# Output projection: a fifth pair of tiles in place of tiles 8 and 9, single steps for the down weights, four buffers for their sums

## The chip, the core and the metric

The kernel runs on one core of one Trainium2 chip. The metric is device time in microseconds (us), as the median of several runs. Engines are named as in the profile: PE (TensorE, matmul), PEld (its weight load), DVE (VectorE), ACT (ScalarE), POOL (GpSimd), SP (SyncE, which here only issues DMAs; SPq is its queue).

## What is computed

The input is one sequence of S = 2048 rows of D = 640. A layer norm feeds two branches whose product is added to the input.

```python
x = A_x
xn = _layernorm(x, axis=-1)
s = _A_ref(xn, A_wqkv, A_wo)
g = _silu(_B_ref(xn, B_w_gate, B_w_up, B_w_down))
return x + s * g
```

Branch A is an attention with 32 heads of 20 columns over 8 positions (every second row back), followed by the output projection `o @ wo` with a 640 x 640 matrix. Branch B is a gated bilinear layer, `((xn @ w_gate) * (xn @ w_up)) @ w_down`, with F = 1536.

```python
attn = _softmax(logits, axis=-1)
o = jnp.einsum("bhsw,bhswd->bhsd", attn, vg)
return (lambda x, *d: x.transpose(*d))(o, 0, 2, 1, 3).reshape(B, S, D) @ wo
```

## The kernel before

**Stages.** The 2048 rows are 16 tiles of 128. First come the norm, the products for q, k, v, the attention on DVE, and the gate and up products (to about 557 us of the span). Then comes the output projection of all 16 tiles (to about 626 us), which is the stage that the change touches. Last come the products with `w_down`, in seven half products for each pair of tiles, with the gate and the output.

**Precision.** A matrix is split in a high part (a copy in the matmul's format, by ACT) and a low part (the matrix less the high part, by DVE or POOL; `split`, L84). A product is then three: high by high, high by low, low by high. The low part of the data comes last, so `mm3` (L91) needs it only for the last third of its matmuls.

**Two forms of the output projection.** Tiles 0 to 7 run as four pairs (`pair_product`, L771). A pair is a 2 x 2 block product done in seven products (numbered 0 to 6, "product (p, j)" for pair p) in place of eight, over 4 of the 5 row blocks of `wo`; the fifth block is added to four of them. A product is 6 matmuls of 320 columns, or 9 with the fifth block. The products accumulate in three PSUM banks, "ACACABA"; the first three are copied to `o` by ACT in between, and a product that adds to the same bank comes behind that copy. Tiles 8 to 15 run singly (`out_proj`, L513): two halves of 15 matmuls of 320 columns each, each evicted by ACT.

**What has to be ready.** For a pair: `load_pair` (four DMAs on SP's queue), `turn_pair` on DVE (two transposes and four sums of 256 columns, L738 to L741), and three high parts (`hi_pair`, ACT) and low parts (`lo_pair`, DVE): part 0 of the first tile, part 2 of the sums S1, S2, S4, part 1 of the second tile. For a single tile: a load (`load_o`), one transpose (`turn_o`, L485), and a high and a low part (`split_o`, L500).

**The down weights beside it.** In the same stage `w_down` is prepared for the last one: 6 blocks k, each in two steps (k, 0) and (k, 1). A step has two sums on DVE (`sum_wd`: L561 and L562, or L566 and L567) and then three or four splits (`split_wd`), high on ACT and low on POOL, 42 in all. The sums T1, T2 stand in tiles of the tag `lg` (two buffers), T4 in `e` (one), so a sum waits until POOL has read what stood there. The attention's logits and two kept products of the last stage use the tag `lg` too.

**Order.** Every engine works its instructions in the order in which the program writes them; nothing is reordered. In pairs 0 to 3 there were 1, 1, 1 and 2 steps of the down weights, and one with each single tile 8 to 14. The tile names that stand in the rows below: `o`, `gs`, `hs` hold outputs on their way to memory, `ot` transposed data, `t` loaded data, `wf` high and low parts, `xc` and `kv` large areas that the down weights and the parts of the pairs share.

Of the kernel before, what the change touches and what calls it, by code (L numbers as in the profile page):

```python
# [37 lines left out]
SCALE = DH ** -0.5  # L38
MASKED = -1e9 / SCALE
EPS = 1e-5  # L40
SP = NT // 2
PAIRS = range(0, W, 2)
PACE = 1.0

# [7 lines left out]
def kernel(  # L52
# [23 lines left out]
    def st(shape, tag, bufs, dt=F32):  # L76
        cnt[0] += 1
        return sb.tile(shape, dt, tag=tag, bufs=bufs, name=f"{tag}_{cnt[0]}")
# [243 lines left out]
    def attention(u):  # L322
        g, r = UN[u]
        nh = GROUPS[g]
        c = nh * DH
        q, kv = q_t[u], kv_t[u]
        pair, one, small = [(n + 155) / 950 for n in (2 * NE * c, NE * c, NE * nh * W)]
        lg = st([P, NE * nh, W], "lg", 2)
        e = st([P, NE * nh, W], "e", 1)
        yield 1.0  # L330

        def places(a, j):

            y = kv[:, a, j:j + NE, :].rearrange("p i c -> p (i c)")
            return bass.AP(y.tensor, y.offset, [y.ap[0], [c, 2], y.ap[1]])

        def pair_tile():
            return st([P, 2, NE * c], "t", 2)

        def heads(y):  # L340
            return y.rearrange("p a (n d) -> p a n d", d=DH)

        for j in PAIRS:
            t = pair_tile()
            nc.vector.tensor_mul(t, q.rearrange("p i c -> p (i c)").unsqueeze(1).to_broadcast([P, 2, NE * c]),  # L345
                                 places(0, j))
            yield pair
            nc.vector.tensor_reduce(out=lg[:, :, j:j + 2].rearrange("p n a -> p a n"), in_=heads(t),  # L348
                                    op=ALU.add, axis=AX.X)
            yield pair  # L350
        m0 = lg[0:1].rearrange("p (i h) w -> p i h w", h=nh)
        nc.vector.tensor_add(m0, m0, mask.unsqueeze(2).to_broadcast([1, NE, nh, W]))
        sm = st([P, 2, NE * nh], "sm", 2)
        nc.vector.tensor_reduce(out=sm[:, 0, :], in_=lg, op=ALU.max, axis=AX.X)
        nc.vector.tensor_sub(lg, lg, sm[:, 0, :].unsqueeze(2).to_broadcast([P, NE * nh, W]))
        yield 3 * small
        nc.scalar.activation(e, lg, AF.Exp, scale=SCALE)
        yield small
        nc.vector.tensor_reduce(out=sm[:, 0, :], in_=e, op=ALU.add, axis=AX.X)
        nc.vector.reciprocal(sm[:, 1, :], sm[:, 0, :])  # L360
        nc.vector.tensor_mul(e, e, sm[:, 1, :].unsqueeze(2).to_broadcast([P, NE * nh, W]))
        yield 3 * small

        def weighted(j, t):
            pw = e[:, :, j:j + 2].rearrange("p n a -> p a n").unsqueeze(3).to_broadcast([P, 2, NE * nh, DH])
            nc.vector.tensor_mul(heads(t), pw, heads(places(1, j)))  # L366

        acc, t = pair_tile(), pair_tile()
        weighted(PAIRS[0], acc)
        yield pair  # L370
        for j in PAIRS[1:]:
            weighted(j, t)
            yield pair
            nc.vector.tensor_add(acc, acc, t)  # L374
            yield pair
        o = st([P, NE, c], "o", 1)
        nc.vector.tensor_add(o.rearrange("p i c -> p (i c)"), acc[:, 0, :], acc[:, 1, :])
        yield one
        for b in range(NQ):
            c0, c1 = max(GOFF[g], b * QC), min(GOFF[g] + c, (b + 1) * QC)  # L380
            if c0 < c1:
                nc.sync.dma_start(o_scr[r, b, :, :, c0 - b * QC:c1 - b * QC].rearrange("s p c -> p s c"),
                                  o[:, :, c0 - GOFF[g]:c1 - GOFF[g]])
# [116 lines left out]
    def split_o(s, y):  # L500
        if s == NT - 2:
            oT[s] = st([P, KD, P], "hs", 2, F32R), st([P, KD, P], "hs", 2, F32R)
        else:
            if s == SP:
                z = blocks(wd_kv["B22"], 4, 2, KD)
            else:
                z = st([P, 2, KD, P], *(("wf", 4) if s < NT - 2 else ("t", 2)), F32R)
            oT[s] = z[:, 0], z[:, 1]
        split(nc.vector, y, *oT[s])
# [46 lines left out]
    def sum_wd(k, part):  # L556
        r = wd_raw[k]
        if part == 0:
            v = wd_v[k] = {"B11": r[:, 0, 0], "B21": r[:, 1, 0], "B22": r[:, 1, 1]}
            v["T1"], v["T2"] = st([P, HALF], "lg", 2), st([P, HALF], "lg", 2)  # L560
            nc.vector.tensor_sub(v["T1"], r[:, 0, 1], r[:, 0, 0])  # L561
            nc.vector.tensor_sub(v["T2"], r[:, 1, 1], v["T1"])  # L562
        else:
            v = wd_v[k]
            v["T4"], v["T3"] = st([P, HALF], "e", 1), r[:, 0, 1]
            nc.vector.tensor_sub(v["T3"], r[:, 1, 1], r[:, 0, 1])  # L566
            nc.vector.tensor_sub(v["T4"], r[:, 1, 0], v["T2"])  # L567
# [89 lines left out]
    def gather(m):  # L657

        n, j = divmod(m, 7)
        a, b = 2 * n, 2 * n + 1  # L660
        p = bank["ACACABA"[j]]
        if j == 0:
            keep("M1", p, "lg", 2)
        elif j == 1:
            keep("M5", p, "lg", 2)
        elif j == 2:
            keep("U2", p, "e", 1)
        elif j == 3:
            g_t[a] = st([P, D], "q", 2)
            nc.vector.tensor_add(g_t[a][:, HALF:], kept["U2"], p)  # L670
            return lambda: silu(a, 1)
        elif j == 4:
            g_t[b] = st([P, D], "q", 2)
            nc.vector.tensor_add(g_t[b][:, HALF:], kept["M5"], p)
            return lambda: silu(b, 1)
        elif j == 5:
            nc.vector.tensor_add(g_t[a][:, :HALF], kept["M1"], p)
            return lambda: silu(a, 0)
        else:
            return lambda: silu(b, 0, p)  # L680
        return lambda: None
# [61 lines left out]
    def hi_pair(p, part):  # L743

        if part == 2:
            if p % 2:
                z = [st([P, 2, KD, P], "wf", 4, F32R).rearrange("p a k c -> p (a k) c")[:, :3 * KS] for _ in range(2)]
            else:
                z = blocks(wd_kv["T4"], 2, 2, 3 * KS) if p else blocks(wd_big[0], 1, 2, 3 * KS)
                z = [z[:, 0], z[:, 1]]  # L750
            raw = pair_raw[p]
        else:
            y, r = (wd_big[3], 3) if p % 2 else (wd_kv["B22"], 2) if p else (wd_kv["T4"], 1)
            z = blocks(y, r, 2, 2 * KD)
            z = [z[:, i, part * KD:(part + 1) * KD] for i in range(2)]
            raw = pair_y[p][:, part]
        pair_z[p, part] = z, raw
        nc.scalar.activation(z[0], raw, AF.Copy)
# [219 lines left out]
    pair_k.append(st([P, 3, HALF], "o", 1))  # L978
    wd_steps = [(k, part) for k in range(KH) for part in range(2)]

    def wd_sums(n):
        for k, part in wd_steps[:n]:
            sum_wd(k, part)

    def wd_splits(n):
        for k, part in wd_steps[:n]:
            split_wd(k, part)
            if part and k + 2 < KH:
                load_wd(k + 2)
        del wd_steps[:n]  # L990

    pair_product(0, 0)
    for p in range(SP // 2):
        more = p + 1 < SP // 2
        n = (1, 1, 1, 2)[p]
        if not more:
            y8 = turn_o(SP)
        wd_sums(n)
        pair_product(p, 1)
        if more:  # L1000
            hi_pair(p + 1, 0)
            lo_pair(p + 1, 0)
        else:
            split_o(SP, y8)
        pair_product(p, 2)
        if more:
            hi_pair(p + 1, 2)
        pair_product(p, 3)
        if more:
            lo_pair(p + 1, 2)  # L1010
            hi_pair(p + 1, 1)
        pair_product(p, 4)
        wd_splits(n)
        if more:
            lo_pair(p + 1, 1)
        pair_product(p, 5)
        if p == 0:
            load_pair(3)
        elif p == 1:
            load_o(SP, 3, st([P, 3, D], "t", 2))  # L1020
            turn_pair(3)
        elif p == 2:
            load_o(SP + 3, 3, st([P, 3, D], "t", 2))
        if more:
            pair_product(p + 1, 0)
        else:
            out_proj(SP, 0)
        pair_product(p, 6)
    n_prod = 7 * NT // 2
    for s in range(SP, NT):  # L1030
        if s + 1 < NT:
            trans_o(s + 1)
        if s == SP + 2:
            load_o(SP + 6, 2, st([P, 2, D], "t", 2))
        wd_sums(1)
        if s > SP:
            out_proj(s, 0)
        out_proj(s, 1)
        wd_splits(1)
        if s == 12:  # L1040
            load_h(0, ("A11", "A21", "A12"))
        elif s == 13:
            load_h(0, ("A22",))
        if s == 14:
            hi_h(0)
            lo_h(0)
# [76 lines left out]
```

## Time and profile before

| what | value |
|---|---|
| median of 3 runs | 779.98 us (779.87 to 781.29) |
| profiled execution | 779.86 us |
| its span | 778.0 us, granted TensorE clock 0.999 |
| output projection, first to last start of L783 | 557.9 to 591.9 us |
| single tiles to the first half product | 588.7 to 625.7 us |

The profile shows one execution. A row of the timeline is: start in us from the span's start, duration in us, engine, line, operation, written tile <- read tiles, shape and number of instructions; in brackets the idle time of the engine just before it and what ended it. Ends of neighbouring rows of one engine overlap by up to 0.1 us on DVE, ACT and POOL, since the next instruction starts while the last one drains; a matmul's row shows its latency, and the next one starts about 0.15 us later. A row of the windows is: stretch, its length, busy time and count for PE, PEld, DVE, ACT and POOL, the granted clock, the busy share of the DMA engines and GB/s.

### The profile page before, as it was taken

How to read it: one execution, taken by the hardware profiler on the slowest of the kernel's cores; microseconds unless marked ns; L12 is line 12 of the kernel's file. 1: busy time of each engine (PE TensorE's matmuls, PEld its weight loads, DVE VectorE, ACT ScalarE, POOL GpSimd, SP SyncE). 2: the span in 40 equal slices, each digit the busy share in tenths (PEclk: the TensorE clock that was granted, in tenths of full speed). 3: DMA queues.
4: the chain of work that ended last, by engine and by line, in shares of the span. 5: the costliest groups of instructions: out<-in, count | busy, mean ns of one | idle time of the engine just before them, and what ended most of it. 6: DMA issues, size and time to landing. Idle time of an engine off the chain costs nothing.

```text
span 778.0 us, 11229 instructions
## 1 busy us (share of the span) xinstructions
PE 770.3 (99%) x4408; PEld 704.1 (91%) x4408; DVE 694.6 (89%) x731; ACT 236.0 (30%) x537; POOL 151.4 (19%) x114
## 2 busy tenths in 40 slices
PE   8999999999999999999999999999999999999997
PEld 6989888898989898989898989888899999999997
DVE  7999898999999999996999999999996787777775
ACT  4323312031112121311121212023455664444442
POOL 5200401022013201120205002042557720000000
PEclk9999999999999999999999999999999999999999
DMA  8562131331224122323023131344467664555533
GB/s 321 172 199 75 43 96 38 96 90 48 85 50 124 49 64 82 111 70 79 29 87 100 44 106 39 113 137 104 138 198 226 201 264 165 200 184 183 183 102 135
DMA packets 82252, 93.97 MB, mean 121 GB/s; under 512 B 23112, under 2 KB 63384, under 8 KB 82072
## 3 DMA queue, kind: packets, MB, share of 16 engines
q1 hardware_dynamic: 82200, 93.27, 38.6%
q8 instruction: 34, 0.56, 0.3%
q14 instruction: 18, 0.15, 0.1%
HBM read 55.84 MB, written 28.31 MB: 108 GB/s over the span
## 4 chain that ended last, share of the span: by engine, by line
PE 98%; DMA 1%; ACT 0%; SPq 0%; DVE 0%; issue 0%
PE q L311 27%; PE u L96 22%; PE g L96 22%; PE q L654 11%; PE u L654 5%; PE q L96 5%; PE g L654 3%; PE q L783 2%; PE u L783 1%; PE g L783 1%; DMA wraw<-in_wqkv 1%; SPq L136 0%; PE q L238 0%; ACT wqh L86 0%; DVE q L640 0%
## 5 line engine op out<-in xcount | busy, mean ns | idle before, releaser
L96 PE MATMUL u<-xc,wf 128*128 128x512 f32 (+1 forms) x735 | 175.8, 390 | 0.0
L96 PE MATMUL g<-xc,wf 128*128 128x512 f32 (+1 forms) x735 | 175.8, 390 | 0.0
L96 PEld LDWEIGHTS u<-xc,wf 128*128 128x128 f32 x735 | 136.4, 188 | 31.0
L96 PEld LDWEIGHTS g<-xc,wf 128*128 128x128 f32 x735 | 136.0, 188 | 29.9
L311 PE MATMUL q<-wqh,xc 128*128 128x300 f32 (+1 forms) x960 | 160.1, 309 | 0.9 <-ACT xc L239 0.9
L311 PEld LDWEIGHTS q<-wqh,xc 128*128 128x128 f32 x960 | 146.2, 188 | 3.0 <-ACT xc L239 1.2
L345 DVE TENSOR_TENSOR t<-q,kv 128x1600 f32<-128x1600 f32 (+1 forms) x48 | 97.0, 2020 | 7.9 <-ACT gs L414 6.9
L87 POOL TENSOR_TENSOR wf<-wraw,wf 128x256 fp32r<-128x256 f32 (+2 forms) x22 | 49.8, 2279 | 266.7 <-ACT wf L86 266.7
L366 DVE TENSOR_TENSOR t<-e,kv 128x1600 f32<-128x1600 f32 (+1 forms) x48 | 97.6, 2051 | 1.1
L348 DVE TENSOR_REDUCE lg<-t 128x80 f32<-128x1600 f32 (+1 forms) x48 | 92.6, 1930 | 1.1
L414 ACT ACTIVATE gs<-g 128x512 f32<-128x512 f32 x48 | 28.7, 599 | 203.2 <-PE g L96 186.0
L311 PE MATMUL q<-wql,xc 128*128 128x300 f32 (+1 forms) x480 | 86.0, 309 | 0.0
L374 DVE TENSOR_TENSOR t<-t,t 128x1600 f32<-128x1600 f32 (+1 forms) x36 | 76.5, 2125 | 1.0
L313 ACT ACTIVATE kv<-q 128x200 f32<-128x200 f32 (+1 forms) x96 | 33.4, 348 | 141.9 <-PE q L311 141.9
L311 PEld LDWEIGHTS q<-wql,xc 128*128 128x128 f32 x480 | 74.2, 188 | 0.0
L654 PE MATMUL q<-xc,wf 128*128 128x320 f32 x432 | 67.2, 308 | 0.0
L87 POOL TENSOR_TENSOR wql<-wraw,wqh 128x300 fp32r<-128x300 f32 (+4 forms) x14 | 34.1, 2461 | 168.4 <-ACT wqh L86 168.4
L654 PEld LDWEIGHTS q<-xc,wf 128*128 128x128 f32 x432 | 64.3, 188 | 0.0
L425 DVE TENSOR_TENSOR hs<-u,gs 128x512 f32<-128x512 f32 x47 | 32.1, 682 | 0.7 <-issue 0.7
L87 POOL TENSOR_TENSOR xc<-wraw,xc 128x320 fp32r<-128x320 f32 (+1 forms) x22 | 28.0, 1274 | 22.9 <-ACT xc L86 22.5
L314 ACT ACTIVATE q<-q 128x100 f32<-128x100 f32 (+1 forms) x96 | 24.6, 256 | 0.0
L617 DVE TENSOR_TENSOR wf<-t,wf 128x768 fp32r<-128x768 f32 x16 | 15.3, 958 | 8.2 <-ACT wf L613 7.5
(259 smaller groups left out, 906.8 us busy)
## 6 DMA issues: line engine op xcount, KB each, us to landing
h_scr<-hs SPq DMA_DIRECT2D x48, 256.0 KB, 2.2
wraw<-in_wgu SPq DMA_DIRECT2D x12, 640.0 KB, 4.9
t<-h_scr SPq DMA_DIRECT2D x8, 768.0 KB, 6.9
hs<-s_scr SPq DMA_DIRECT2D x16, 320.0 KB, 3.7
gs<-in_x SPq DMA_DIRECT2D x16, 320.0 KB, 4.1
out<-q SPq DMA_DIRECT2D x14, 320.0 KB, 2.6
wraw<-h_scr SPq DMA_DIRECT2D x11, 384.0 KB, 5.6
wraw<-in_wd SPq DMA_DIRECT2D x12, 320.0 KB, 3.8
```

Source lines behind the costliest of these rows:

```text
L87: eng.tensor_sub(lo, raw, hi.bitcast(F32))
L96: nc.tensor.matmul(acc, a, b, start=first and n == 0, stop=last and n == len(runs) - 1)
L311: nc.tensor.matmul(p, xT[(r * NE + i) // TPC][a][:, k, t0:t0 + P], wq[g][b][:, k], start=n == 0, stop=n == len(runs) - 1, skip_group_check ...
L313: nc.scalar.activation(kv_t[u][:, :, W - 1 + i, :], p[:, c:].rearrange("p (a c) -> p a c", a=2), AF.Copy)
L345: nc.vector.tensor_mul(t, q.rearrange("p i c -> p (i c)").unsqueeze(1).to_broadcast([P, 2, NE * c]), places(0, j))
L348: nc.vector.tensor_reduce(out=lg[:, :, j:j + 2].rearrange("p n a -> p a n"), in_=heads(t), op=ALU.add, axis=AX.X)
L366: nc.vector.tensor_mul(heads(t), pw, heads(places(1, j)))
L374: nc.vector.tensor_add(acc, acc, t)
L414: nc.scalar.activation(gs, pp[0], AF.Copy)
L425: nc.vector.tensor_mul(hs, pp[1], gs)
L654: nc.tensor.matmul(p, y[:, i, k], wd_t[name][k][:, l], start=new and r == 0, stop=r == len(runs) - 1, skip_group_check=True)
L783: nc.tensor.matmul(b, y, w, start=new and r == 0, stop=r == len(runs) - 1, skip_group_check=True)
```

## The change

The constant that ends the pairs goes from 8 to 10, so tiles 8 and 9 become pair 4, and tiles 10 to 15 stay single. Pair 4's parts 0 and 1 get places of their own in the shared areas, its part 2 takes two buffers of `wf` (which pair 3 had), and its high part stands one product later for that reason. `lg` gets four buffers. The steps of the down weights are no longer taken in a number for each pair, but one at a time, with splits taking whatever sums are done: (0,0), (0,1), (1,0), (1,1) in pairs 0 to 3, (2,0) at the end of pair 3, (2,1) and (3,0) in pair 4, (3,1) with tile 10, and one for each of the tiles 11 to 14. The loads of single tiles are two of three tiles (10 to 12, 13 to 15) in place of 3, 3 and 2.

```diff
-SP = NT // 2
+SP = 10
...
-        lg = st([P, NE * nh, W], "lg", 2)
+        lg = st([P, NE * nh, W], "lg", 4)
...
-            if p % 2:
+            if p % 2 or p > 3:
                 z = [st([P, 2, KD, P], "wf", 4, F32R).rearrange("p a k c -> p (a k) c")[:, :3 * KS] for _ in range(2)]
...
-            y, r = (wd_big[3], 3) if p % 2 else (wd_kv["B22"], 2) if p else (wd_kv["T4"], 1)
-            z = blocks(y, r, 2, 2 * KD)
-            z = [z[:, i, part * KD:(part + 1) * KD] for i in range(2)]
+            y, r = (wd_big[3], 3) if p % 2 else (wd_kv["T4"], 1) if p == 0 else (wd_kv["B22"], 2 if p == 2 else 4)
+            if p > 3 and part:
+                y, r = wd_big[2], 2
+            z = blocks(y, r + 2 * part, 2, KD)
+            z = [z[:, i] for i in range(2)]
...
-    def wd_sums(n):
-        for k, part in wd_steps[:n]:
-            sum_wd(k, part)
-
-    def wd_splits(n):
-        for k, part in wd_steps[:n]:
+    to_split = []
+
+    def wd_sums():
+        if wd_steps:
+            to_split.append(wd_steps.pop(0))
+            sum_wd(*to_split[-1])
+
+    def wd_splits():
+        while to_split:
+            k, part = to_split.pop(0)
             split_wd(k, part)
             if part and k + 2 < KH:
                 load_wd(k + 2)
-        del wd_steps[:n]
...
     for p in range(SP // 2):
         more = p + 1 < SP // 2
-        n = (1, 1, 1, 2)[p]
         if not more:
-            y8 = turn_o(SP)
-        wd_sums(n)
+            y1 = turn_o(SP)
+        if p < 3:
+            wd_sums()
         pair_product(p, 1)
         if more:
             hi_pair(p + 1, 0)
             lo_pair(p + 1, 0)
+            if p == 3:
+                wd_sums()
         else:
-            split_o(SP, y8)
+            split_o(SP, y1)
         pair_product(p, 2)
-        if more:
+        if not more:
+            wd_splits()
+            wd_sums()
+        elif p < 3:
             hi_pair(p + 1, 2)
         pair_product(p, 3)
         if more:
+            if p == 3:
+                hi_pair(p + 1, 2)
             lo_pair(p + 1, 2)
             hi_pair(p + 1, 1)
         pair_product(p, 4)
-        wd_splits(n)
+        wd_splits()
         if more:
             lo_pair(p + 1, 1)
         pair_product(p, 5)
         if p == 0:
             load_pair(3)
         elif p == 1:
-            load_o(SP, 3, st([P, 3, D], "t", 2))
+            load_pair(4)
             turn_pair(3)
         elif p == 2:
-            load_o(SP + 3, 3, st([P, 3, D], "t", 2))
+            load_o(SP, 3, st([P, 3, D], "t", 2))
+            turn_pair(4)
+        else:
+            if p == 3:
+                load_o(SP + 3, 3, st([P, 3, D], "t", 2))
+            wd_sums()
...
     for s in range(SP, NT):
         if s + 1 < NT:
             trans_o(s + 1)
-        if s == SP + 2:
-            load_o(SP + 6, 2, st([P, 2, D], "t", 2))
-        wd_sums(1)
+        wd_sums()
         if s > SP:
             out_proj(s, 0)
         out_proj(s, 1)
-        wd_splits(1)
+        wd_splits()
```

The other places where `lg` had two buffers (`sum_wd`, `gather`) have four too, and the parts of tile 10 stand where pair 1's and pair 3's stood.

More of the change, by code (lines that the diff above doesn't have):

```diff
@@ L504, in split_o @@
             if s == SP:
-                z = blocks(wd_kv["B22"], 4, 2, KD)
+                z = blocks(wd_big[3], 4, 2, KD)
             else:
@@ L559, in sum_wd @@
             v = wd_v[k] = {"B11": r[:, 0, 0], "B21": r[:, 1, 0], "B22": r[:, 1, 1]}
-            v["T1"], v["T2"] = st([P, HALF], "lg", 2), st([P, HALF], "lg", 2)
+            v["T1"], v["T2"] = st([P, HALF], "lg", 4), st([P, HALF], "lg", 4)
             nc.vector.tensor_sub(v["T1"], r[:, 0, 1], r[:, 0, 0])
@@ L662, in gather @@
         if j == 0:
-            keep("M1", p, "lg", 2)
+            keep("M1", p, "lg", 4)
         elif j == 1:
-            keep("M5", p, "lg", 2)
+            keep("M5", p, "lg", 4)
         elif j == 2:
```

## The prediction

> **What bounds the kernel now.** I read the shares of the engines first, then the chain of waits, then windows over the stage that is changed, then the timeline of each engine there.
>
> ```profile
> PE 770.3 (99%) x4408; PEld 704.1 (91%) x4408; DVE 694.6 (89%) x731; ACT 236.0 (30%) x537; POOL 151.4 (19%) x114
> PE 98%; DMA 1%; ACT 0%; SPq 0%; DVE 0%; issue 0%
> 601.31:610.11 8.80, 8.80 (x62) 8.80 (x61) 6.70 (x8) 5.40 (x13) 6.85 (x8) 1.00 0.76 224
> 616.91:625.71 8.80, 8.80 (x61) 8.80 (x61) 5.82 (x8) 5.52 (x13) 6.87 (x8) 1.00 0.52 188
> ```
>
> TensorE sets the end: 98% of the chain is its matmuls. The two windows (length, then PE, PEld, DVE, ACT, POOL busy, clock, DMA) lie in the single tiles of the output projection: PE is full at clock 1.00, DVE and POOL are each busy 65% to 78%. A busy PE does not show a short wait, so the starts of its matmuls are read:
>
> ```profile
> 590.02 0.30 PE L96 MATMUL q<-q,kv 128*128 128x320 f32 x1
> 590.29 0.56 PE L96 MATMUL q<-wf,kv 128*128 128x320 f32 x2
> 590.70 0.31 PE L96 MATMUL q<-wqh,kv 128*128 128x320 f32 x1
> 625.73 2.80 PE L654 MATMUL q<-xc,wf 128*128 128x320 f32 x18
> 628.36 2.80 PE L654 MATMUL u<-xc,wf 128*128 128x320 f32 x18
> ```
>
> Eighteen matmuls take 628.36 - 625.73 = 2.63 us, 0.146 each. The three from 590.02 to 590.70 took 0.68 where 0.44 were due: PE lost **0.24 us** in tile 8. Its cause on DVE:
>
> ```profile
> 583.88 0.48 DVE L561 TENSOR_TENSOR lg<-wraw 128x320 f32<-128x320 f32 x1
> 587.67 1.15 DVE L562 TENSOR_TENSOR lg<-wraw,lg 128x320 f32<-128x320 f32 x1 [3.31 <-POOL xc L87]
> 588.75 1.49 DVE L87 TENSOR_TENSOR kv<-ot,kv 128x640 fp32r<-128x640 f32 x1
> ```
>
> The sum T2 waited 3.31 us for POOL to leave an `lg` buffer, tile 8's low part (L87, DVE) came behind it and ended at 588.75 + 1.49 = 590.24, and PE went on at 590.29.
>
> **The change part by part.** *Tiles 8 and 9 as a pair.* Removed are 60 matmuls of 320 columns (two halves of 15, two tiles), added 54 (42 in seven products, 12 for the fifth row block). The time between like evictions prices both forms as they run here:
>
> ```profile
> 575.28 0.44 ACT L797 ACTIVATE hs<-q 128x320 f32<-128x320 f32 x1 [0.88 <-PE q L783]
> 583.16 0.44 ACT L797 ACTIVATE hs<-q 128x320 f32<-128x320 f32 x1 [0.57 <-PE q L783]
> 599.32 0.44 ACT L520 ACTIVATE hs<-q 128x320 f32<-128x320 f32 x1 [1.58 <-PE q L96]
> 603.76 0.44 ACT L520 ACTIVATE gs<-q 128x320 f32<-128x320 f32 x1 [1.40 <-PE q L96]
> ```
>
> A pair takes 583.16 - 575.28 = 7.88 us, a single tile 603.76 - 599.32 = 4.44. Two tiles are 8.88, so the pair saves **1.00 us**; six matmuls at 0.146 give 0.88, the lower bound.
>
> *Four `lg` buffers.* The 3.31 us wait goes, and with it PE's **0.24 us**. In the attention and in the last stage, which use the same buffers, PE waits for no `lg`, so more of them change nothing; if that cover were gone, nothing would be dearer than before.
>
> *The fifth pair's own preparation.* DVE gets a `turn_pair` (two transposes, four sums of 256) at the end of pair 2, ACT three high parts, DVE three low parts, SP a load of two tiles in the place of one of three, on the same queue behind the same store.
>
> ```profile
> 574.13 1.98 SPq L479 DMA_DIRECT2D t<-o_scr  x4
> 581.95 0.83 DVE L485 STREAM_TRANSPOSE ot<-t 128x640 f32<-128x640 f32 x1
> 573.60 1.56 DVE L485 STREAM_TRANSPOSE ot<-t 128x640 f32<-128x640 f32 x2
> 577.14 0.48 DVE L561 TENSOR_TENSOR lg<-wraw 128x320 f32<-128x320 f32 x1
> 576.51 0.73 ACT L758 ACTIVATE xc<-ot 128x640 fp32r<-128x640 f32 x1
> 586.04 1.04 PE L783 MATMUL q<-xc,xc 128*128 128x320 f32 x6
> ```
>
> The load issued at 574.13 was there by 581.95; the new one is smaller, at the same place. `turn_pair` of pair 3 took 577.14 - 573.60 = 3.54, so pair 4's runs from 581.95 to about 585.5, in time in which DVE before waited for `lg` until 587.67: nothing on PE. ACT's first high part of pair 3 ran at 576.51, before `turn_pair` was through, so it needs the first transpose only. The part S1/S2/S4 of pair 4 reuses pair 3's buffer, and so waits for product (3,3); product (3,4) starts at 586.04, so (3,3) is through about 586.3. With 0.8 on ACT, 1.0 on DVE and DVE's own queue it is ready near 588.6; product (4,1) comes 33 matmuls after 586.04, at 590.9. Nothing, then; were these 2.3 us gone, PE would wait for it one to one.
>
> *Where the next thing is late.* In the last pair ACT's queue has the high part of tile 10 ahead of the eviction of product (4,2), and (4,4) accumulates in that bank. The high part waits for tile 10's transpose, which DVE now does behind the two sums of step (2,0). Walking DVE from 585.5 with the durations of the rows (three low parts, three additions out of PSUM, two split sums while POOL works) I get the transpose done at 592.9, the eviction at 594.05 and (4,4), 54 matmuls after 586.04, due at 593.9: **+0.1 us**, bounds 0 (DVE half a microsecond earlier) and 1.0 (every DVE instruction behind a POOL one).
>
> *The down weights in single steps.* Step (3,0)'s three and (3,1)'s four splits are now issued together behind tile 10. What a tile costs on DVE when POOL works beside it is in these rows:
>
> ```profile
> 597.45 0.83 DVE L87 TENSOR_TENSOR wf<-ot,wf 128x640 fp32r<-128x640 f32 x1 [1.26 <-ACT wf L86]
> 598.20 1.17 DVE L561 TENSOR_TENSOR lg<-wraw 128x320 f32<-128x320 f32 x1
> 599.45 1.00 DVE L562 TENSOR_TENSOR lg<-wraw,lg 128x320 f32<-128x320 f32 x1
> 602.07 1.48 DVE L87 TENSOR_TENSOR wf<-ot,wf 128x640 fp32r<-128x640 f32 x1 [0.86 <-ACT wf L86]
> 603.48 0.48 DVE L566 TENSOR_TENSOR wraw<-wraw 128x320 f32<-128x320 f32 x1
> 603.88 0.48 DVE L567 TENSOR_TENSOR e<-wraw,lg 128x320 f32<-128x320 f32 x1
> 604.28 0.83 DVE L485 STREAM_TRANSPOSE ot<-t 128x640 f32<-128x640 f32 x1
> ...
> 596.63 0.88 POOL L87 TENSOR_TENSOR xc<-lg,xc 128x320 fp32r<-128x320 f32 x1
> 597.47 1.54 POOL L87 TENSOR_TENSOR xc<-wraw,xc 128x320 fp32r<-128x320 f32 x1
> 598.98 1.12 POOL L87 TENSOR_TENSOR kv<-e,kv 128x320 fp32r<-128x320 f32 x1
> 604.64 0.88 POOL L87 TENSOR_TENSOR xc<-wraw,xc 128x320 fp32r<-128x320 f32 x1 [1.77 <-ACT xc L86]
> 607.82 1.13 POOL L87 TENSOR_TENSOR kv<-e,kv 128x320 fp32r<-128x320 f32 x1
> ...
> 599.66 0.46 ACT L86 ACTIVATE xc<-wraw 128x320 fp32r<-128x320 f32 x1
> 600.02 0.46 ACT L86 ACTIVATE kv<-wraw 128x320 fp32r<-128x320 f32 x1
> 601.30 0.74 ACT L86 ACTIVATE wf<-ot 128x640 fp32r<-128x640 f32 x1 [0.46 <-DVE ot L485]
> 605.54 0.73 ACT L86 ACTIVATE wf<-ot 128x640 fp32r<-128x640 f32 x1
> ```
>
> POOL's instruction of 597.47 came just behind DVE's low part and took 1.54 where 0.88 is usual; DVE's L561 took 1.17 (0.48 alone, row 577.14) and ended 0.36 after it; the next POOL one again. They take turns, each waiting for the other's whole instruction. From one low part (597.45) to the end of the next high part (601.30 + 0.74) it takes **4.59 us + r**, r the rest of a POOL instruction that the low part meets (0 there; 1.48 - 0.83 = 0.65 at 602.07). A tile whose sums are L566/L567 had no POOL beside them (POOL idle 1.77 before 604.64), and took two POOL turns of 0.73 less.
>
> Now the new order, E being the end of tile 10. ACT evicts at E + 0.21, starts the seven splits 0.34 later at 0.36 each (599.32, 599.66, 600.02), so tile 12's high part runs from E + 3.07 to E + 3.81. PE wants it at E + 4.44: 0.63 spare (in before hi of tile 12 ended at 606.27 where ACT's eviction rhythm puts the need at about 608.0: 1.7 spare). POOL starts the seven at about E + 1.1 and, with DVE's turns between, ends them at E + 8 to 8.3; before it ended the four of (3,1) at 607.82 + 1.13 = 608.95, that is 5.4 after tile 10's end. So POOL runs some 2.7 us late, and the idle 1.77 that let L566/L567 pass alone is gone. Tiles 13, 14 and 15 then cost DVE 4.59 + r each against PE's 4.44: the loss is 3 x 0.15 + (sum of r) - 0.63 = sum of r - 0.2. With r = 0 to 0.75 three times: **-0.2 (none) to +2.05**; I take r = 0.45, so **+1.2**, nearer the 0.65 row than 0, as POOL is seldom idle here.
>
> The Trainium skill (SBUF — State Buffer, section "SBUF: two separate sides") says that a VectorE instruction with two SBUF inputs and a GpSimd one take an exclusive lock on the shared port pair for the whole instruction, and the loser fully blocks. The trace agrees (1.17 against 0.48). If they shared the port in proportion instead, a low part would lose a fraction whenever it came, r would be near its mean of both ends and the phase would not matter; by the lock it is decided by who comes first, and the sum lies anywhere between the bounds above.
>
> At the start of the half products the same can happen once more:
>
> ```profile
> 625.68 1.62 DVE L601 TENSOR_TENSOR wqh<-ot,wraw 128x768 f32<-128x768 f32 x1
> 627.34 1.84 ACT L613 ACTIVATE wf<-wqh 128x768 fp32r<-128x768 f32 x2 [0.98 <-DVE wqh L601]
> ```
>
> The first of the two conversions ends near 628.2, product 1 begins at 628.36: 0.15 spare. POOL's last step a little later relative to PE costs **+0.1** (0 to 0.7).
>
> Sum against the profiled execution, 778.0 span and 779.86 in all, which the 1.86 around the span leaves unchanged: 779.86 - 1.00 - 0.24 + 0.1 + 1.2 + 0.1 = 780.0. The median of the runs, 779.98, is 0.12 above that execution: **780.15 us**.
>
> **The rivals.** *Clean gain.* POOL catches up before tile 13, or r is small each time: 779.98 - 1.24 = 778.75 (to 779.3 with a rest of 0.5). For it: DVE and POOL are each below 80% busy. Against: it needs the low r three times running.
> *Slower than before by over 0.2%.* The alternation of DVE and POOL reaches through all three tiles with r near 0.75, (4,4) pays its 1.0 and product 1 its 0.7: -1.24 + 2.05 + 1.0 + 0.7 = +2.5, so 782.5. It decides from a total PE wait of 2.8 us on. For it: the seven splits wait as a block and r was 0.65 in the B tiles. Against: each wait of PE gives POOL time to catch up.
> *The pair saves nothing because a load is late.* Tile 10's transpose has its load one pair earlier, as tile 8's had; `load_pair(4)` has 581.95 - 576.11 = 5.8 after its last issue. If it came 1 us late the slack of pair 4 would take it; 2 us late gives about 780.9. For it only that DMA is busy 0.5 to 0.8 there.
>
> **How the numbers follow.** Forecast (part of the gain eaten, 779.3 to 781.5) 0.58; clean gain 0.22; slower 0.14; late load 0.06. 0.2% of the median is 1.56 us, about what a measurement of this kernel tells from no change: faster means below 778.42, which the largest gain misses by 0.3 (0.05 for spread of runs), slower above 781.54 (rival two and the tail of the forecast, 0.15), within 0.80. The range is the forecast with the clean gain below it and half of the way to the slower case above: 778.6 to 781.8.
>
> **What would show it.** Right: no wait of L562 for POOL; L96 240 - 60 = 180 and the pair's line 270 matmuls; seven POOL instructions without a pause after tile 10; L566/L567 of the next step at 0.8 to 1.2 instead of 0.48; PE waits, each below 1 us, at the first matmuls of tiles 13 to 15 behind ACT's high part. Wrong: PE gaps in products (3,4) to (4,3), a transpose that waits for a load, L566/L567 at 0.48, or no gap at all in the tiles 13 to 15 (then the clean gain).

## The result and the profile after

The changed kernel takes 780.82 us (median of 22 runs, 780.18 to 784.83) where the kernel before takes 779.95 (22 runs on the same chip): ratio 1.0015, 95% interval 1.0009 to 1.0021. That is a loss of 0.9 us by the medians, which alone would give 1.0011. It is below the 0.2% that the prediction took as the least to be called a change, but the interval leaves out 1, so the sign is clear. The executions of one kernel fall into groups some 0.5 us apart (for the kernel before 779.34 to 779.63 and 779.87 to 780.07), so below, a small difference of medians is read together with the stage lengths of the profiles. The profiled execution took 780.93 us with a span of 779.1; before it was 779.86 and 778.0.

The shares of the engines after:

```profile
PE 770.2 (99%) x4402; PEld 703.4 (90%) x4402; DVE 700.1 (90%) x739; ACT 237.4 (30%) x538; POOL 152.8 (20%) x114
```

TensorE has six matmuls fewer (4402 for 4408) and is as busy as before, 770.2 for 770.3: what six matmuls gave back went somewhere in which PE counts as busy. DVE has eight instructions and 5.5 us more (700.1 for 694.6), but is not the engine that sets the end.

The starts of the matmuls say it. Timeline of PE after, first the start of the stage, then the last matmul of a tile and the first three of the next (for the tiles 13, 14 and 15), then the half products:

```profile
557.96 1.05 PE L785 MATMUL q<-wf,kv 128*128 128x320 f32 x6
...
611.18 0.31 PE L96 MATMUL q<-q,wf 128*128 128x320 f32 x1
611.44 0.56 PE L96 MATMUL q<-wf,wf 128*128 128x320 f32 x2
611.84 0.31 PE L96 MATMUL q<-wqh,wf 128*128 128x320 f32 x1
...
615.84 0.31 PE L96 MATMUL q<-q,wf 128*128 128x320 f32 x1
616.65 0.56 PE L96 MATMUL q<-wf,hs 128*128 128x320 f32 x2 [0.50 <-ACT hs L86]
617.05 0.31 PE L96 MATMUL q<-wqh,hs 128*128 128x320 f32 x1
...
621.09 0.31 PE L96 MATMUL q<-q,hs 128*128 128x320 f32 x1
621.89 0.56 PE L96 MATMUL q<-wf,t 128*128 128x320 f32 x2 [0.50 <-ACT t L86]
622.29 0.31 PE L96 MATMUL q<-wqh,t 128*128 128x320 f32 x1
...
626.40 2.80 PE L654 MATMUL q<-xc,wf 128*128 128x320 f32 x18
629.05 2.92 PE L654 MATMUL u<-xc,wf 128*128 128x320 f32 x18
631.80 0.31 PE L654 MATMUL q<-xc,wf 128*128 128x320 f32 x1
```

From the first to the third row of each group it should be 0.44 (three matmuls at 0.146). It is 0.66, 1.21 and 1.20, so PE lost 0.22, 0.77 and 0.76 there; with 0.10 more where tile 14's low part is first used (618.21 to 618.60 for two matmuls), the three tiles lost **1.85 us**. Only part of it has a wait written beside it (twice 0.50); the rest hides inside the modelled ends of the matmuls. The half product that was due 2.64 after 629.05 began 2.75 after it, 0.11 more. From its first matmul to half product 0 the stage lasts 626.40 - 557.96 = 68.44 us; before it was 67.85 (557.88 to 625.73).

Why PE waited stands on the other three engines. ACT after (the eviction that frees the bank of product (4,4), the eviction that ends tile 10, and the high parts of tiles 12 to 15), then DVE, then POOL:

```profile
593.51 0.42 ACT L788 ACTIVATE o<-q 128x320 f32<-128x320 f32 x1
602.68 0.44 ACT L520 ACTIVATE gs<-q 128x320 f32<-128x320 f32 x1 [1.14 <-PE q L96]
605.54 0.72 ACT L86 ACTIVATE wf<-ot 128x640 fp32r<-128x640 f32 x1
610.65 0.74 ACT L86 ACTIVATE wf<-ot 128x640 fp32r<-128x640 f32 x1 [1.43 <-DVE ot L485]
615.86 0.74 ACT L86 ACTIVATE hs<-ot 128x640 fp32r<-128x640 f32 x1 [0.28 <-DVE ot L485]
621.11 0.74 ACT L86 ACTIVATE t<-ot 128x640 fp32r<-128x640 f32 x1 [1.37 <-DVE ot L485]
```

```profile
591.98 0.85 DVE L485 STREAM_TRANSPOSE ot<-t 128x640 f32<-128x640 f32 x1 [0.16 <-DMA t<-o_scr]
...
606.30 1.33 DVE L87 TENSOR_TENSOR wf<-ot,wf 128x640 fp32r<-128x640 f32 x1 [2.33 <-ACT wf L86]
607.55 1.16 DVE L561 TENSOR_TENSOR lg<-wraw 128x320 f32<-128x320 f32 x1
...
611.42 1.47 DVE L87 TENSOR_TENSOR wf<-ot,wf 128x640 fp32r<-128x640 f32 x1 [0.87 <-ACT wf L86]
612.82 1.16 DVE L566 TENSOR_TENSOR wraw<-wraw 128x320 f32<-128x320 f32 x1
613.90 1.17 DVE L567 TENSOR_TENSOR e<-wraw,lg 128x320 f32<-128x320 f32 x1
...
616.63 1.52 DVE L87 TENSOR_TENSOR hs<-ot,hs 128x640 fp32r<-128x640 f32 x1 [0.80 <-ACT hs L86]
```

```profile
603.55 0.89 POOL L87 TENSOR_TENSOR xc<-wraw,xc 128x320 fp32r<-128x320 f32 x1 [2.18 <-ACT xc L86]
...
609.41 1.13 POOL L87 TENSOR_TENSOR kv<-e,kv 128x320 fp32r<-128x320 f32 x1
...
625.72 1.59 POOL L87 TENSOR_TENSOR kv<-e,kv 128x320 fp32r<-128x320 f32 x1
```

Read them from top to bottom as one story. Tile 10 ends at 602.68 - 0.21 = 602.47. POOL has stood idle for 2.18 us, gets its first input at 603.55, and then runs the seven splits without a pause to 609.41 + 1.13 = 610.54. POOL runs on into tile 15 with no pause but 0.22 us ahead of 617.68. Beside it DVE's low parts cost 1.33 to 1.52 instead of 0.83, and the sums 1.05 to 1.17 instead of 0.48. Neither number is new by itself: before, a tile paid for the one or for the other (0.83 with 1.17 and 1.00 from 597.45 on, 1.48 with twice 0.48 from 602.07 on, in the rows of the prediction). What is new is that the same tile pays for both, since L566 and L567, which before slipped through at 0.48 each while POOL was idle, now cost 1.16 and 1.17. A low part and its two sums take 3.5 to 3.8 us in all where they took 2.4 to 3.0. So tile 13's transpose is late, so ACT's high part of it is late (it ends at 610.65 + 0.74 = 611.39), and PE begins tile 13 at 611.44. Tiles 14 and 15 follow the same way: 616.60 and 616.65, 621.85 and 621.89.

### The profile page after: what moved, and what is told of

Read it like the earlier page. It is cut to its first block, busy times and chain, and to the rows that moved or that the text cites. A ratio compares the mean times of both kernels' runs of the same rounds, so it can differ in the third digit from the quotient of the medians.

```text
span 779.1 us, 11232 instructions
## 1 busy us (share of the span) xinstructions
PE 770.2 (99%) x4402; PEld 703.4 (90%) x4402; DVE 700.1 (90%) x739; ACT 237.4 (30%) x538; POOL 152.8 (20%) x114
## 4 chain that ended last, share of the span: by engine, by line
PE 97%; DVE 2%; issue 1%; ACT 0%; DMA 0%; DVEq 0%; ACTq 0%
PE q L311 27%; PE u L96 22%; PE g L96 22%; PE q L654 11%; PE u L654 5%; PE q L785 3%; PE g L654 3%; PE q L96 2%; PE u L785 1%; PE g L785 1%; DVE ot L485 0%; DMA t<-in_xb 0%; DVE stats L187 0%; DVE lg L561 0%; DVE wraw L566 0%
```

## The experiments

The shares leave two explanations. *Theory:* the gain of the pair and of the four `lg` buffers is real, and comes back as waits because the seven splits start in one block behind tile 10, on a POOL that was idle just before; DVE and POOL take turns (each instruction with two inputs waits for the other engine's), and the chain from a low part to the next high part grows longer than PE's 4.44 us. *Rival A:* the pair never saved anything. *Rival B:* the four buffers themselves cost something. Inside the theory a second question opened: is it DVE's chain alone, or does POOL's lateness cost by itself?

**Splits of step (3,0) as soon as their sums are there.** Against the changed kernel:

```diff
         else:
             out_proj(SP, 0)
+            wd_splits()
         pair_product(p, 6)
```

> The changed kernel with one more call of the splits behind tile 10's first half, so that step (3,0)'s three splits come before, and (3,1)'s four behind, tile 10's second half. Theory (DVE and POOL take turns, and PE's waits before tiles 13, 14, 15 come from POOL being some 2.7 us late behind the batch of seven): POOL starts (3,0) at once behind (2,1), near 601.4, the idle 2.18 us before 603.55 goes, L566/L567 of step (4,1) take 0.48 or one of them does, the PE waits of 0.2, 0.9 and 0.8 us before tiles 13, 14, 15 shrink to less than 0.4 in sum, and the time falls by 1.4 to 1.8 us from 780.8 to 779.0 to 779.4, which is below the kernel before. Rival (a single tile simply costs DVE more than PE's 4.44 us, wherever the splits stand): the waits stay above 1.2 us in sum, 780.3 to 780.8.

Measured: 779.39 us (778.83 to 780.79) against 779.50 for the kernel before in the same set, ratio 0.9996 [0.9987, 1.0004]; compared with the changed kernel's 1.0015 the loss is gone. POOL in this kernel, around the end of tile 10 (the first row is the last split of (2,1), the second the first of (3,0), the third the last of the seven):

```profile
599.55 0.87 POOL L87 TENSOR_TENSOR kv<-e,kv 128x320 fp32r<-128x320 f32 x1
600.39 0.87 POOL L87 TENSOR_TENSOR xc<-wraw,xc 128x320 fp32r<-128x320 f32 x1
...
606.50 1.46 POOL L87 TENSOR_TENSOR kv<-e,kv 128x320 fp32r<-128x320 f32 x1
```

It has no pause, and the seven end at 607.96 instead of 610.54. What is left of the waits lies ahead of tile 13: 611.03 - 610.48 is 0.40 more than the 0.15 due, and with the next two matmuls it is 0.50 in all for 1.85:

```profile
610.48 0.31 PE L96 MATMUL q<-q,wf 128*128 128x320 f32 x1
611.03 0.56 PE L96 MATMUL q<-wf,wf 128*128 128x320 f32 x2 [0.24 <-ACT wf L86]
...
624.41 2.80 PE L654 MATMUL q<-xc,wf 128*128 128x320 f32 x18
```

No instruction is added or removed by this edit, only three splits are issued sooner, and the stage is 68.44 - 67.10 = 1.34 us shorter (557.31 to 624.41). The time is where it was expected; the waits are 0.50 where less than 0.4 was expected. That speaks for the theory, against both rivals as the main cause, and against the rival that a single tile costs DVE too much wherever the splits stand. It does not tell the two forms of the theory apart: the edit starts POOL sooner, and it also gives ACT three conversions less ahead of tile 12's high part, which gives DVE's chain a head start.

**POOL writes and reads nothing.** In steps (4,0), (4,1) and (5,0) the low part of each block is a fill of the whole block with zeros instead of a subtraction, so that POOL still works beside DVE but reads no SBUF (these ten blocks are then zero in the output):

```diff
         for name in (("B11", "B22", "T1"), ("B21", "T2", "T3", "T4"))[part]:
+            if (k, part) in ((4, 0), (4, 1), (5, 0)):
+                nc.scalar.activation(wd_t[name][k][:, 0], wd_v[k][name], AF.Copy)
+                nc.gpsimd.memset(wd_t[name][k].bitcast(F32), 0.0)
+                continue
             split(nc.gpsimd, wd_v[k][name], ...)
```

> The changed kernel in which steps (4,0), (4,1) and (5,0) have, in the place of POOL's low part, a POOL fill with zeros over high and low part (so these ten blocks of down weights are zero in the output); each still waits for ACT's high part, and POOL reads no SBUF in it. Theory (the low parts and sums of DVE wait for POOL's reads): beside the fills the low part of tile 13 takes 0.83 in place of 1.47, L566 and L567 of (4,1) 0.48 in place of 1.16, L561 and L562 of (5,0) about 0.5 in place of 1.1, the PE waits before tiles 14 and 15 go and that of 0.2 before tile 13 stays: 780.8 - 1.6 = 779.2. Rival (DVE is slowed by anything that POOL does, or the waits come from POOL being late alone): the DVE durations stay, the waits stay, 780.6 to 780.9 if a fill takes 0.85 or more.

Measured: 778.94 us (778.46 to 780.26), ratio 0.9992 [0.9983, 1.0001]; the stage takes 66.82. DVE, then POOL, in this kernel ahead of tile 14:

```profile
610.96 0.82 DVE L87 TENSOR_TENSOR wf<-ot,wf 128x640 fp32r<-128x640 f32 x1 [0.87 <-ACT wf L86]
611.70 0.48 DVE L566 TENSOR_TENSOR wraw<-wraw 128x320 f32<-128x320 f32 x1
612.11 0.48 DVE L567 TENSOR_TENSOR e<-wraw,lg 128x320 f32<-128x320 f32 x1
```

```profile
610.59 0.64 POOL L573 MEMSET kv<- 128x640 f32 x1
611.16 0.64 POOL L573 MEMSET xc<- 128x640 f32 x1
612.00 1.78 POOL L573 MEMSET xc<- 128x640 f32 x3 [0.20 <-ACT xc L572]
```

POOL is at work beside all three DVE instructions, but for a gap of 0.20 ahead of 612.00, and they take what they take alone: 0.82, 0.48, 0.48, where beside subtractions the same three took 1.47, 1.16 and 1.17. The waits of tiles 14 and 15 are gone. So it is not POOL being busy that stretches DVE here but POOL reading; of the instructions that read nothing only a fill was tried. One caveat: a fill comes every 0.57 to 0.64 us and a subtraction every 0.84, so POOL is also less late here; the durations are the clean part of this run, the time is not.

**Two `lg` buffers in the changed kernel, four in the kernel before.** The same edit in both directions, in all five places (`"lg", 4` to `"lg", 2`, and back):

> The changed kernel with two buffers of lg in place of four. From the rows of the changed kernel the sums of (4,0) and (5,0) come after POOL has read what stood two steps before; only the second sum of (3,0) would wait, from 597.92 to about 599.7, which leaves tile 11's high part 0.2 later at most, with over a microsecond to spare. So: no difference, 780.6 to 781.0, and no PE wait that the changed kernel does not have. Rival (the four buffers are needed for the single steps, as without them DVE's wait of 3.3 us comes back): a PE wait of 0.24 us or more in tile 10 or 11, 781.0 to 782.5.

> The kernel before with four buffers of lg and nothing else. Theory: DVE's wait of 3.31 us before L562 goes, tile 8's low part is ready in time, PE's 0.24 us there go, and nothing else moves: 0.2 to 0.3 us faster than before, near the limit of what the times tell, and seen in the starts of PE's matmuls. Rival (the wait only moves: POOL and DVE meet elsewhere): the 0.24 us come back within the next tiles, 0.0 to 0.2 slower or the same.

Measured: the changed kernel with two buffers 780.85 us, ratio to before 1.0019 [1.0010, 1.0027], as with four. The kernel before with four takes 779.49 against 779.50, ratio 1.0004 [0.9994, 1.0013]: the 0.2 to 0.3 us that were expected do not show in the times. The profile of the second shows them: DVE's T2 in tile 8, which took 1.15 behind a wait of 3.31 before, and PE's first and last row of the stage:

```profile
584.25 0.49 DVE L562 TENSOR_TENSOR lg<-wraw,lg 128x320 f32<-128x320 f32 x1
```

```profile
557.79 1.05 PE L783 MATMUL q<-wf,kv 128*128 128x320 f32 x6
...
625.37 2.80 PE L654 MATMUL q<-xc,wf 128*128 128x320 f32 x18
```

The stage takes 67.58, 0.27 less than before. In the changed kernel the buffers are worth nothing: with two, the stage takes 68.41 against 68.44, and L562 of step (3,0) waits 0.77 for POOL without PE noticing. The long wait of T2 does not come back there, so it is the new order, with the fifth pair and the single steps, that took it away. Rival B falls.

**Tile 12's high part ahead of the seven splits.** If DVE's chain were the whole cause, giving it tile 12's high part seven conversions (7 x 0.36 = 2.5 us) sooner should do as well as the first experiment:

```diff
-        if s + 1 < NT:
+        if s + 1 < NT and s + 1 not in oT:
             trans_o(s + 1)
         wd_sums()
...
         out_proj(s, 1)
+        if s == SP:
+            trans_o(s + 2)
         wd_splits()
```

> The changed kernel with tile 12's transpose, high and low part ahead of the seven splits of (3,0) and (3,1) in place of behind them. POOL then starts the seven 1.6 us later still (about 605.2 in place of 603.55), as ACT waits about 1 us for tile 12's transpose. Theory (PE waits only for the chain low part, sums, transpose, high part from tile to tile, which gets some 1.4 us of room): tile 13's high part ends near 609.5 in place of 611.4, no PE wait above 0.3 us in tiles 12 to 15, and the time falls by 1.3 to 1.8 us, to 779.0 to 779.5, though POOL is later than in the changed kernel. Rival (POOL being late is the cause in itself): waits as large as in the changed kernel or larger, 780.8 to 782.

Measured: 780.94 us, ratio 1.0017 [1.0009, 1.0026]: no gain at all, and the expectation fails. POOL, DVE and PE in this kernel:

```profile
604.97 1.16 POOL L87 TENSOR_TENSOR xc<-wraw,xc 128x320 fp32r<-128x320 f32 x1 [4.06 <-ACT xc L86]
```

```profile
620.49 1.53 DVE L87 TENSOR_TENSOR t<-ot,t 128x640 fp32r<-128x640 f32 x1 [0.81 <-ACT t L86]
621.95 1.16 DVE L566 TENSOR_TENSOR wraw<-wraw 128x320 f32<-128x320 f32 x1
```

```profile
619.87 0.31 PE L96 MATMUL q<-q,hs 128*128 128x320 f32 x1
620.51 0.56 PE L96 MATMUL q<-wf,t 128*128 128x320 f32 x2 [0.34 <-ACT t L86]
...
625.49 2.91 PE L654 MATMUL q<-xc,wf 128*128 128x320 f32 x18 [0.22 <-ACT wf L613]
629.06 2.91 PE L654 MATMUL u<-xc,wf 128*128 128x320 f32 x18 [0.66 <-ACT wf L613]
```

The waits of tiles 13 and 14 did go, tile 15 still loses 620.51 - 619.87 - 0.15 = 0.49 at its start (0.70 in all), half product 0 loses 0.38, and the stage is 0.74 shorter than in the changed kernel (67.70). But POOL now starts 1.42 later, its last split of the stage ends at 627.31 as it did in the changed kernel, and half product 1 begins 629.06 - 625.49 = 3.57 after half product 0 instead of 2.64. The wait has moved across the end of the stage: from its start to half product 2 it is 74.01 us here and 73.84 in the changed kernel. The DVE rows show how the head start is lost. Tile 15's low part begins 1.38 sooner (620.49 for 621.87), but in the changed kernel POOL stood idle there for 1.87, and here it does not: the low part takes 1.53 for 0.83 and L566 1.16 for 0.48, together 1.38, so L567 begins at 623.03 for 623.02. So POOL's lateness is a cause of its own: giving DVE a head start alone only chooses where PE pays.

**Tiles prepared two ahead, and with it the early splits.** The first kernel transposes tile s + 2 ahead of the sums and splits it behind tile s (the diff); the second has the early splits of the first experiment as well:

```diff
     for s in range(SP, NT):
-        if s + 1 < NT:
+        if s == SP:
             trans_o(s + 1)
+        if s + 2 < NT:
+            y1 = turn_o(s + 2)
         wd_sums()
...
         out_proj(s, 1)
+        if s + 2 < NT:
+            split_o(s + 2, y1)
         wd_splits()
```

> The changed kernel with the preparation of the single tiles one tile further ahead: tile s + 2 is transposed before the sums of tile s, and its high and low part stand behind tile s and ahead of the splits. The chain from tile to tile then no longer holds the sums and the splits, while POOL and DVE have the same work. Theory: no PE wait in tiles 11 to 15 at all, although L561 to L567 are as long as in the changed kernel (1.0 to 1.2); product 0 starts 1.7 to 1.9 us earlier, 778.9 to 779.2. Rival (DVE and POOL together have too much in the single tiles, so that a reorder only moves the waits): waits of 0.5 us or more come back in tile 14 or 15 or at half products 0 and 1, 779.6 to 780.8.

> Step (3,0)'s splits early and the preparation two tiles ahead, together. Theory: there is nothing left to win behind the second once PE waits nowhere, so the same time as with the preparation alone, 778.8 to 779.2, and both below the kernel before by 0.7 to 1.1 us, which is the pair's 1.0 and tile 8's 0.24 less what is left at the half products. Rival (POOL's lateness costs more at the half products): 0.3 us or more below the version with the preparation alone.

Measured: two ahead 779.52 us, ratio 0.9996 [0.9983, 1.0008]; both edits **778.81 us** (778.07 to 780.16) against 779.83 for the kernel before, ratio 0.9982 [0.9974, 0.9991]. PE and POOL with two ahead alone:

```profile
627.19 3.08 PE L654 MATMUL u<-xc,wf 128*128 128x320 f32 x18
630.10 2.80 PE L654 MATMUL q<-xc,wf 128*128 128x320 f32 x18
...
635.73 2.80 PE L654 MATMUL q<-xc,wf 128*128 128x320 f32 x18
```

```profile
626.65 1.60 POOL L87 TENSOR_TENSOR kv<-e,kv 128x320 fp32r<-128x320 f32 x1
```

and with both edits:

```profile
557.19 0.61 PE L785 MATMUL q<-wf,kv 128*128 128x320 f32 x3
...
623.81 2.80 PE L654 MATMUL q<-xc,wf 128*128 128x320 f32 x18
626.45 2.80 PE L654 MATMUL u<-xc,wf 128*128 128x320 f32 x18
```

```profile
622.98 1.60 POOL L87 TENSOR_TENSOR kv<-e,kv 128x320 fp32r<-128x320 f32 x1
```

Two ahead alone takes all waits out of the tiles (stage 66.62), as its theory said. But POOL ends at 628.25, and half products 1 to 3 together give back 635.73 - 627.19 - 3 x 2.64 = 0.62 (the first of it 630.10 - 627.19 = 2.91 for 2.64), and 779.52 is slower than the 778.9 to 779.2 of that theory, just short of its rival's range. With both edits POOL ends at 624.58, half product 1 follows at 2.64, and the stage takes the same 66.62. I had expected the two kernels to be equal by my theory of DVE's chain, and the second 0.3 or more faster by the rival that POOL's lateness costs at the half products; it is 0.7 faster by the medians, the half products show 0.62 of it, and the rival was right, though the two intervals against the kernel before overlap. Rival A falls too: this kernel has the pair, and its stage is 0.96 shorter than that of the kernel before with four buffers (67.58), which has no pair 4 and no PE wait in the tiles either. It is the version that beats both kernels, by some 0.2%.

## Why the prediction was right

The time (780.15 forecast, 780.82 measured) is inside the range, and the likeliest case, a part of the gain eaten, is what happened. The range is no strong test: 778.6 to 781.8 has the kernel before in its middle and so leaves even the sign open. (Its upper end is not what its words give either, as half of the way from 781.5 to 782.5 is 782.0; 780.82 lies inside both.) What speaks for the prediction is that the waits stand where they were said to stand, behind ACT's high parts of the tiles 13 to 15 and each below 1 us, with POOL's seven instructions without a pause and L566 and L567 at 1.16 and 1.17. The steps, in the prediction's order:

- *The pair saves 1.00.* Right: the kernel before with four buffers and the kernel with both edits have no PE wait in the tiles, and their stages differ by 67.58 - 66.62 = 0.96.
- *Four `lg` buffers save 0.24.* Right as an effect in the kernel before (0.27). In the changed kernel the term belongs to the new order and not to the buffers, which are worth nothing there (780.85 with two, 780.82 with four). The two savings together, from before to the kernel with both edits, are 67.85 - 66.62 = 1.23 where 1.24 were forecast.
- *The fifth pair's own preparation costs nothing.* Right, as far as the 0.96 shows it.
- *Product (4,4) +0.1.* It cost 0: tile 10's transpose ran at 591.98 to 592.83 as walked (592.9), and the eviction ended at 593.93; (4,4) began at 594.13, straight behind the product ahead of it. The one wait for a load that the late-load rival spoke of is there, 0.16 us, and nothing follows from it.
- *Tiles 13 to 15 +1.2.* The mechanism was right, its **size** was not: 1.85. The walk up to tile 12 held to a few hundredths (high part from E + 3.07 to E + 3.79, POOL from E + 1.08 to E + 8.07, against 3.07, 3.81, 1.1 and 8 to 8.3). The mis-sized term is r, the rest of a POOL instruction that a low part meets. I took 0.45 three times; the low parts of 1.33, 1.47 and 1.52 give, less 0.83, 0.50, 0.64 and 0.69. By the prediction's own formula that makes 1.83 - 0.2 = 1.63. The other 0.2 is not slack: tile 12's high part ended at 606.26 and PE began that tile at 606.89, 0.63 later as forecast. About 0.09 is that a tile without a wait takes PE 4.41 here (606.89 - 602.48, the first matmuls of the tiles 12 and 11), not 4.44, three times over. The other 0.11 comes behind the end of the chain, in tile 15: the two matmuls behind the wait take 0.40 (621.89 to 622.29) where 0.29 is due.
- *Half product 1 +0.1.* Right: 0.11.

The terms as measured add up to -0.96 - 0.27 + 0 + 1.85 + 0.11 = +0.73. The profiles show 0.59 in the stage and 0.13 behind it to the last half product, 0.72. The profiled spans differ by 1.1: 0.08 lies ahead of the stage, and 0.3 behind the last instruction of DVE, which ends the kernel at 775.51 + 0.49 while the span ends 3.1 later, in the last store. That rest was not looked into.

The term of the tiles was 0.65 low, and r carries 0.48 of that (1.83 for three times 0.45). The prediction named a reason for a high r (POOL seldom idle) and then took the middle. One may think that DVE and POOL keep in step from tile to tile, so that three like values were to be expected rather than three independent ones around a mean; that fits the three numbers and was not tested. A busy POOL alone does not make r high: in the kernel with both edits the low parts at 611.82 and 616.26 took 0.94 and 0.98 with POOL idle for no more than 0.15 beside them, so r was 0.11 and 0.15.

The clean gain fell for the reason given against it. It exists, as 778.81, with the splits early enough that POOL does not fall behind, and the tiles prepared two ahead. The slower case was nearer than the forecast made it: 1.85 of the 2.8 us from which it was to decide.

## What to carry to other kernels

When work for two engines that read the same memory is put together into one block, ask when the later of the two starts and what it did just before: here, using POOL's 2.18 us of idle time ahead of the block took the loss away (1.34 us of the stage). Look past the end of the stage: a head start for one engine of such a pair moved waits to the half products, and of the four kernels that moved instructions without changing them, the two that started the late one sooner had none there. On a bound engine that counts as 99% busy, a loss of 1 to 2 us showed in the spacing of instruction starts and in stage lengths, not in the busy share.

## What the hardware showed that I had not expected

A fill on GpSimd, which only writes, did not disturb DVE: 0.48 us for L566 and L567 beside fills, 1.16 and 1.17 beside subtractions of half the size. The prediction spoke of POOL working beside DVE; what counted here is whether POOL reads. The Trainium skill (SBUF — State Buffer, section "SBUF: two separate sides") has it so: a VectorE instruction with two SBUF inputs takes the lock only against a GpSimd one that reads SBUF. The runs agree, as far as a fill can show it.

The contention does not stand in the trace as a wait. L567 of 1.17 us carries no releaser; it is simply 0.69 longer than the same instruction elsewhere. Where waits were printed, as in POOL's 2.18 and 4.06 behind ACT, they belong to semaphores. It is found by comparing an instruction's duration with its own shortest one.

Not tried: a second buffer for `e`, for which L567 waited in two of these kernels (0.78 us with tile 12's high part first), and a sixth pair.
